# Raw weight tiles into larger free slots, three buffers for q, k and v, loads in written order, ScalarE's decoding in program order

## The chip, the cores and the metric

The kernel runs on one core of a Trainium2 chip. The metric is device time in microseconds (us): the median of three runs, with the lowest and the highest. The profile is of one further execution.

Five engines share the work: TensorE (PE, with its weight loads as PEld), VectorE (DVE), ScalarE (ACT), GpSimd (POOL) and SyncE (SP), which here only issues the DMAs. Each takes its instructions in the order in which the built program has them.

## The reference

Attention over 4 batches of 8 heads, 576 positions of 64 values each. A score is kept where it is within tau = 0.02 of its row's largest; the rest get weight 0. Then two matrix products of a gated layer, one more, and a second layer of two:

```python
scores = scale * np.matmul(q, k.transpose(0, 1, 3, 2))
thresh = np.max(scores, axis=-1, keepdims=True) - tau
scores = np.where(scores >= thresh, scores, -1000000000.0)
scores = scores - np.max(scores, axis=-1, keepdims=True)
attn = np.exp(scores)
attn = attn / (np.sum(attn, axis=-1, keepdims=True) + 1e-09)
x = np.matmul(attn, v)          # then heads side by side: 2304 x 512
...
h = (x @ w1) * (x @ w2) @ w3    # 512 -> 1024, then 1024 x 1024
x = h @ w_out                   # 1024 -> 512
...
h = x @ w_in                    # 512 -> 2048
out = np.maximum(0.01 * h, h) @ w_out2
```

All of it is float32. The weights reach the core as 64-bit integers that hold float64 bits: their size in memory is twice that of float32.

## The kernel before

**Weights.** A weight tile of 128 partitions by 1024 values is loaded in two *halves* of 512 KB (`st`, three buffers) and decoded to float32. ScalarE scales the high words (`t`, L140) and the low words (`st` in place, L141), VectorE shifts `t` left by three bits (L142), GpSimd adds the two (L145, or L148 into `wt`). A weight for a float32r product is then split in two parts: ScalarE rounds (L149) and GpSimd subtracts (L150). `stream` (L108) issues a staging load for each half that has been decoded; it is called for `first` and later for `w2`. The 20 tiles of `first` are four of `wo`, eight of `w3` and eight of `w12`. The 16 of `w2` follow when attention is over.

**Folding.** `fold_weights` (L338) multiplies `w3` and `wo` into `w34` while attention runs: eight blocks of eight products (`ps34`, L346), a block for each tile of `w3`. With `w34` the gated layer needs two products, `psab` (x by `w12`, L367) and `psh` (L386), both float32r with three passes.

**Attention.** A *unit* is a pair of heads of a batch and one of two groups of rows, g = 0 with two steps or g = 1 with three, of which the first has one head's work for both. There are 8 units in a batch, 32 in all, and 80 steps. A unit's q and k lie in `qk`, its v in `vv`, each with two buffers; `load_unit` issues four to six DMAs on SP. `scale_unit` multiplies q on VectorE (L186). A step is `scores` (PE L207 or L211, VectorE's maximum L217, GpSimd's threshold L218, ScalarE's exponential L219), `mask` (VectorE L233), `transposes` (PE L253 to L268, copies by ScalarE and VectorE), and once per unit `weighted` (PE L283) and `normalise` (PE L313, `x` on GpSimd L317).

**Order.** The main loop (L425) walks the steps and puts into each a share of decoding (`halves += 1.7 * weight`, where a step with two heads weighs 2) and of the gated layer (`rate`). The gated layer of a batch's group starts two steps after its last unit. A scheduler then sets the order on each engine from priorities and its own picture of what is ready; the written order counts only where it leaves a tie, for SP's DMAs as well.

**w2.** After attention `stream` decodes the 16 tiles of `w2` into the slots that are free by then; `up` and `down` (L526, L548) run over five chunks of columns, and the rest of the time is theirs.

## Time and profile before

| | |
|---|---|
| median of 3 runs | 1155.42 us (1151.76 to 1160.67) |
| profiled execution | 1158.23 us, span 1156.4 us |
| TensorE busy | 1081.0 us, 93% |
| VectorE, ScalarE, GpSimd busy | 454.6, 474.3, 322.1 us |
| mean granted TensorE clock | 0.980 |
| moved by DMA | 77.61 MB, 223 GB/s in the first fortieth of the span, 46 GB/s in the middle |

The span runs from the first to the last instruction. Busy times of engines overlap; a wait is idle time with the instruction that ended it. A stretch is a window of time from the span's start. The granted clock is a share of TensorE's full speed, 2.4 GHz; a share between 0.5 and 1 means that a part of the stretch ran at the lower level, 1.2 GHz.

### The profile page before, as it was taken

The numbers are of one execution on the slowest core, as the hardware profiler recorded it, in microseconds if no ns is written. First come the engines' busy times: TensorE is split into PE (matmuls) and PEld (weight loads), VectorE is DVE, ScalarE is ACT, GpSimd is POOL, SyncE is SP. The second block draws the span as 40 slices with busy tenths as digits, with TensorE's granted clock in tenths as the row PEclk, the third lists the DMA queues.
The fourth block names the chain that finished last, engine by engine and source line by source line (L and its number), as shares of the span: only waits on it lengthen the run. The fifth ranks groups of instructions, "written<-read, shape, count | busy, mean of one in ns | idle before, by whom it ended". The sixth has DMA issues, their size and how long they took to land.

```text
span 1156.4 us, 16341 instructions
## 1 busy us (share of the span) xinstructions
PE 1081.0 (93%) x6288; PEld 851.8 (74%) x6288; DVE 454.6 (39%) x887; ACT 474.3 (41%) x891; POOL 322.1 (28%) x456
## 2 busy tenths in 40 slices
PE   2799788999999999989999989999999999999998
PEld 1344466778877788877787768987788888888887
DVE  4454555554554554554554554154321121111111
ACT  4545774344343443443443444257632232222232
POOL 3334972122222121221221216388810010000000
PEclk9799799999999999999999998999999999999999
DMA  7544551111211111111121103245320010010000
GB/s 223 163 117 159 170 173 43 46 53 40 67 40 33 54 54 40 53 41 57 41 61 45 40 10 119 70 147 168 111 73 1 1 64 1 1 46 1 1 37 20
DMA packets 37407, 77.61 MB, mean 67 GB/s; under 512 B 4817, under 2 KB 19665, under 8 KB 37329
## 3 DMA queue, kind: packets, MB, share of 16 engines
q1 hardware_dynamic: 37184, 76.56, 21.7%
q8 instruction: 50, 0.82, 0.3%
q14 instruction: 29, 0.23, 0.1%
q10 hardware_dynamic: 144, 0.00, 0.0%
HBM read 67.11 MB, written 9.44 MB: 66 GB/s over the span
## 4 chain that ended last, share of the span: by engine, by line
PE 72%; DMA 9%; DVE 5%; POOL 5%; ACT 4%; issue 3%; SPq 1%; DVEq 0%; ACTq 0%; POOLq 0%
PE po L548 14%; PE ps L526 14%; PE psab L367 13%; PE psh L386 8%; PE av L283 7%; PE sc L211 6%; DMA qk<-in_qkv 4%; DMA st<-in_w 4%; PE tp L263 4%; PE ps L346 2%; POOL wt L148 2%; PE sc L207 1%; DVE nm L217 1%; PE tq L268 1%; DVE t L142 1%
## 5 line engine op out<-in xcount | busy, mean ns | idle before, releaser
L367 PE MATMUL psab<-x,w 128*128 128x256 f32 (+1 forms) x1536 | 233.6, 303 | 4.6 <-DVE xs L314 1.7
L367 PEld LDWEIGHTS psab<-x,w 128*128 128x128 f32 x1536 | 210.0, 190 | 22.4 <-issue 9.9
L526 PE MATMUL ps<-h,w 128*128 128x512 f32 (+1 forms) x960 | 216.0, 370 | 0.4 <-ACT w L149 0.4
L548 PE MATMUL po<-w,gg 128*128 128x512 f32 x864 | 214.1, 392 | 1.9 <-ACT gg L533 1.8
L526 PEld LDWEIGHTS ps<-h,w 128*128 128x128 f32 x960 | 169.5, 188 | 34.9 <-ACT w L149 1.2
L548 PEld LDWEIGHTS po<-w,gg 128*128 128x128 f32 x864 | 159.7, 188 | 38.0 <-ACT gg L533 4.5
L217 DVE TENSOR_REDUCE nm<-sc 128x1 f32<-128x576 f32 x144 | 108.8, 755 | 186.9 <-PE sc L211 144.2
L534 DVE TENSOR_TENSOR gg<-gf,gg 128x512 fp32r<-128x512 f32 (+1 forms) x80 | 60.4, 756 | 268.9 <-ACT gg L533 268.9
L531 ACT ACTIVATE gf<-ps 128x512 f32<-128x512 f32 (+1 forms) x80 | 44.3, 555 | 226.1 <-PE ps L526 226.0
L219 ACT ACTIVATE e<-sc,nm 128x576 f32<-128x576 f32 x144 | 106.9, 742 | 58.8 <-DVE nm L217 56.9
L263 PE MATMUL tp<-ident,e 128*128 128x128 f32 x512 | 80.8, 282 | 43.2 <-DVE e L233 38.8
L233 DVE SCALAR_TENSOR_TENSOR e<-sc,th,e 128x576 f32<-128x576 f32 x144 | 112.4, 812 | 21.0 <-ACT e L219 21.0
L386 PE MATMUL psh<-gt,w 128*128 128x256 f32 (+1 forms) x768 | 112.6, 301 | 1.9 <-ACT xs L286 1.9
L386 PEld LDWEIGHTS psh<-gt,w 128*128 128x128 f32 x768 | 104.0, 190 | 6.7 <-issue 3.5
L263 PEld LDWEIGHTS tp<-ident,e 128*128 128x128 f32 x512 | 61.6, 145 | 55.5 <-issue 33.6
L218 POOL TENSOR_TENSOR th<-cb,nm 128x1 f32<-128x1 f32 x144 | 27.7, 193 | 231.3 <-DVE nm L217 231.3
L211 PE MATMUL sc<-qk 64*128 64x288 f32 x512 | 83.6, 447 | 6.4 <-DVE qk L186 6.0
L142 DVE TENSOR_SCALAR t<-t 128x512 int32<-128x512 int32 x72 | 55.0, 765 | 79.2 <-ACT t L140 69.5
L378 POOL TENSOR_TENSOR gt<-at,gt 128x256 fp32r<-128x256 f32 (+1 forms) x64 | 52.3, 817 | 103.9 <-ACT gt L377 103.8
L283 PE MATMUL av<-HH,vv 128*64 128x256 f32 (+1 forms) x512 | 73.1, 427 | 0.0
L150 POOL TENSOR_TENSOR w<-wt,w 128x512 fp32r<-128x512 f32 x48 | 66.5, 1400 | 20.4 <-ACT w L149 19.8
L503 POOL TENSOR_TENSOR h<-hr,h 128x1024 fp32r<-128x1024 f32 (+1 forms) x10 | 22.3, 2233 | 173.1 <-DVE h L502 173.1
(67 smaller groups left out, 997.7 us busy)
## 6 DMA issues: line engine op xcount, KB each, us to landing
st<-in_w SPq DMA_DIRECT2D x48, 512.0 KB, 4.3
vv<-in_qkv SPq DMA_DIRECT2D x64, 160.0 KB, 2.3
st<-in_w3t SPq DMA_DIRECT2D x16, 512.0 KB, 3.9
qk<-in_qkv SPq DMA_DIRECT2D x32, 208.0 KB, 3.5
qk<-in_qkv SPq DMA_DIRECT2D x32, 144.0 KB, 2.9
out<-os SPq DMA_DIRECT2D x18, 256.0 KB, 2.2
st<-in_wout SPq DMA_DIRECT2D x8, 512.0 KB, 6.4
hr<-h3d SPq DMA_DIRECT2D x8, 512.0 KB, 3.7
```

Source lines behind the costliest of these rows:

```text
L142: nc.vector.tensor_scalar(out=t, in0=t, scalar1=3, scalar2=None, op0=ALU.logical_shift_left)
L150: nc.gpsimd.tensor_tensor(out=dst[:, 1, sl], in0=f(w), in1=f(dst[:, 0, sl]), op=ALU.subtract)
L211: nc.tensor.matmul(sc[:, a, half, :HS], qk[r, o:o + P], qk[r, ks], start=True, stop=True)
L217: nc.vector.tensor_reduce(out=nm, in_=sc[:, a, :, :HS], op=ALU.max, axis=AX.XY, negate=True)
L219: nc.scalar.activation(e[:, a].rearrange("p (a b) -> p a b", a=2), sc[:, a, :, :HS], AF.Exp, bias=nm)
L233: nc.vector.scalar_tensor_tensor(out=ev, in0=sc[:, a, :, :HS], scalar=th, in1=ev, op0=ALU.is_ge, op1=ALU.mult, accum_out=stat[key][:, o:o ...
L263: nc.tensor.transpose(tp[:, kc], e[:, a, kc * P:kc * P + P], ident)
L283: nc.tensor.matmul(av[a * D:a * D + D, :gw], vv[:, a, kc], rhs, start=(i == 0), stop=(i == NK - 1))
L367: nc.tensor.matmul(ps[:, :gw], w12_t[i][:, a, o:o + P], xt[kk][:, c, :gw], start=(m == 0), stop=(m == 11))
L386: nc.tensor.matmul(ps[:, :gw], w34_t[i // 2][:, a, i % 2, o * P:o * P + P], gt[i][:, c, :gw], start=(m == 0), stop=(m == 23))
L526: nc.tensor.matmul(ps[:, :tw], w2_t[j][:, a, kk * P:kk * P + P], h3_t[ci][:, c, kk, :tw], start=(m == 0), stop=(m == 11))
L548: nc.tensor.matmul(po_t[t], gg[:, c, t * P:t * P + P], w2_t[j][:, a, 512:], start=(j == 0 and (a, c) == PASSES[0]), stop=(j == KF2 - 1 and ...
```

## The change

- The halves of `wo`, `w3` and the first four tiles of `w12` are loaded as whole tiles of 1 MB (`raw`) into slots of `wpool` that are free at the time: tag wB for `wo` and `w3`, wA for `w12`. Up to seven halves beyond the decoded ones are asked for. The last four tiles of `w12`, and `w2`, go through `st` as before.
- The low words get a tile of their own (`lw`); `wt` is gone.
- The float32 tiles of `wo` lie in two slots of wA, `w3` has three buffers instead of two, `qk` and `vv` three.
- Up to the gated layer of the first batch's second group, SP's DMAs keep the written order. `load_unit` is called two units ahead.
- The two decoding instructions on ScalarE are held in program order, and the two halves that were decoded ahead of the first scores are not. The pace of decoding is 1.2 instead of 1.7 halves per unit of weight.
- For `w2`, VectorE does the second half's subtraction, and the tiles are assigned to other slots: the fourth lies in a slot of wB instead of a pool that opens later.

```diff
--- before.py
+++ after.py
@@ -105,51 +105,64 @@
         nc.vector.tensor_tensor(out=cb, in0=cb, in1=neg, op=ALU.subtract)
 
 
-    def stream(jobs, pool, depth):
-        ahead = []
-        todo = [(slot, src, c) for slot, src in jobs for c in range(2)]
-        def issue():
-            if todo:
-                slot, src, c = todo.pop(0)
-                st = pool.tile([P, 1024], I32, tag="st", name="st", bufs=depth)
-                nc.sync.dma_start(out=st, in_=src[:, c * 512:c * 512 + 512].bitcast(I32))
-                ahead.append((slot, c, st))
-        for _ in range(depth):
-            issue()
-        return decode(ahead, issue, pool)
-    def decode(ahead, issue, pool):
-        while ahead:
-            slot, c, st = ahead.pop(0)
-            if c == 0:
-                dst = slot()
-            sl = slice(c * 512, c * 512 + 512)
-            words = st.rearrange("p (c two) -> p c two", two=2)
-            low, high = words[:, :, 0], words[:, :, 1]
-            t = pool.tile([P, 512], I32, tag="t", name="t", bufs=2)
-            nc.scalar.activation(f(t), f(high), AF.Prelu, scale=2.0 ** -112, alpha=-2.0 ** 32)
-            nc.scalar.activation(low, low.bitcast(U32), AF.Copy, scale=2.0 ** -29)
-            nc.vector.tensor_scalar(
-                out=t, in0=t, scalar1=3, scalar2=None, op0=ALU.logical_shift_left)
-            if len(dst.shape) == 2:
-                nc.gpsimd.tensor_tensor(out=dst[:, sl].bitcast(I32), in0=t, in1=low, op=ALU.add)
-            else:
-                w = pool.tile([P, 512], I32, tag="wt", name="wt", bufs=2)
-                nc.gpsimd.tensor_tensor(out=w, in0=t, in1=low, op=ALU.add)
-                nc.scalar.copy(dst[:, 0, sl], f(w))
-                nc.gpsimd.tensor_tensor(out=dst[:, 1, sl], in0=f(w), in1=f(dst[:, 0, sl]), op=ALU.subtract)
-            issue()
-            yield
+    def stream(jobs, by_dve):
+        todo = [(job, c) for job in jobs for c in range(2)]
+        loaded = []
+        state = [0, None]
+        def issue(most=2 * len(jobs)):
+            while len(loaded) < min(most, len(todo)):
+                (slot, src, raw), c = todo[len(loaded)]
+                if len(loaded) >= state[0] + (7 if raw in ("wB", "wC") else 3):
+                    return
+                if raw is None:
+                    st = wld.tile([P, 1024], I32, tag="st", name="st", bufs=3)
+                    nc.sync.dma_start(out=st, in_=src[:, c * 512:c * 512 + 512].bitcast(I32))
+                    loaded.append(st)
+                else:
+                    if c == 0:
+                        state[1] = wpool.tile(
+                            [P, 2, 1024], I32, tag="wB" if raw == "wB" else "wA", name="raw")
+                        nc.sync.dma_start(
+                            out=state[1].rearrange("p c w -> p (c w)"), in_=src.bitcast(I32))
+                    loaded.append(state[1][:, c])
+        def decode():
+            for k, ((slot, src, raw), c) in enumerate(todo):
+                if c == 0:
+                    dst = slot()
+                sl = slice(c * 512, c * 512 + 512)
+                words = loaded[k].rearrange("p (w two) -> p w two", two=2)
+                low, high = words[:, :, 0], words[:, :, 1]
+                t = wld.tile([P, 512], I32, tag="t", name="t", bufs=2)
+                lw = wld.tile([P, 512], I32, tag="lw", name="lw", bufs=2)
+                tc.keep_in_program_order(
+                    nc.scalar.activation(f(t), f(high), AF.Prelu, scale=2.0 ** -112, alpha=-2.0 ** 32))
+                tc.keep_in_program_order(
+                    nc.scalar.activation(lw, low.bitcast(U32), AF.Copy, scale=2.0 ** -29))
+                nc.vector.tensor_scalar(
+                    out=t, in0=t, scalar1=3, scalar2=None, op0=ALU.logical_shift_left)
+                if len(dst.shape) == 2:
+                    nc.gpsimd.tensor_tensor(out=dst[:, sl].bitcast(I32), in0=t, in1=lw, op=ALU.add)
+                else:
+                    nc.gpsimd.tensor_tensor(out=lw, in0=t, in1=lw, op=ALU.add)
+                    nc.scalar.copy(dst[:, 0, sl], f(lw))
+                    eng = nc.vector if by_dve and c else nc.gpsimd
+                    eng.tensor_tensor(out=dst[:, 1, sl], in0=f(lw), in1=f(dst[:, 0, sl]), op=ALU.subtract)
+                state[0] = k + 1
+                yield
+                issue()
+        return decode(), issue
 
     units = [(b * 4 + p, g) for b in range(B) for g in range(2) for p in range(4)]
     qk_t, vv_t = {}, {}
@@ -161,8 +174,8 @@
         pair, g = units[u]
         gq, gw, _ = GROUPS[g]
         b, h = pair // 4, 2 * (pair % 4)
-        qk = apool.tile([P, S + 320], F32, tag="qk", name="qk", bufs=2)
-        vv = apool.tile([P, 2, NK, D], F32, tag="vv", name="vv", bufs=2)
+        qk = apool.tile([P, S + 320], F32, tag="qk", name="qk", bufs=3)
+        vv = apool.tile([P, 2, NK, D], F32, tag="vv", name="vv", bufs=3)
         for a in range(2):
             o = a * D
             src = qkv[b, h + a][o:o + D]
@@ -323,17 +336,21 @@
 
     def slot(table, i, tag, name):
         def make():
-            if tag in ("wA", "wB"):
+            if tag == "w3":
+                table[i] = fold.tile([P, 1024], F32, tag=tag, name=name, bufs=3)
+            elif name == "wo":
+                if i % 2 == 0:
+                    table["both"] = wpool.tile([P, 2, 1024], F32, tag=tag, name=name)
+                table[i] = table["both"][:, i % 2]
+            else:
                 table[i] = wpool.tile([P, 2, 1024], F32R, tag=tag, name=name)
-            else:
-                table[i] = fold.tile([P, 1024], F32, tag=tag, name=name, bufs=4 if tag == "wo" else 2)
             return table[i]
         return make
 
-    first = [(slot(wo_t, t, "wo", "wo"), wout[t]) for t in range(4)]
-    first += [(slot(w3_t, i, "w3", "w3"), w3t[i]) for i in range(KF)]
-    first.insert(2, first.pop(4))
-    first += [(slot(w12_t, i, "wB" if i < 4 else "wA", "w12"), w12[i]) for i in range(KF)]
+    first = [(slot(wo_t, t, "wA", "wo"), wout[t], "wB") for t in range(4)]
+    first += [(slot(w3_t, i, "w3", "w3"), w3t[i], "wB") for i in range(KF)]
+    first += [(slot(w12_t, i, "wB" if i < 4 else "wA", "w12"), w12[i],
+               ("wC", "wA", None, None)[i // 2]) for i in range(KF)]
 
     def fold_weights():
 
@@ -363,9 +380,8 @@
                 m = 0
                 for kk in range(KD):
                     for a, c in PASSES:
-                        o = mat * 512 + kk * P
                         nc.tensor.matmul(
-                            ps[:, :gw], w12_t[i][:, a, o:o + P], xt[kk][:, c, :gw],
+                            ps[:, :gw], w12_t[i][:, a, mat * 512 + kk * P:mat * 512 + kk * P + P], xt[kk][:, c, :gw],
                             start=(m == 0), stop=(m == 11))
                         m += 1
                 if mat == 0:
@@ -399,10 +415,15 @@
             yield from gn
 
 
+    in_order = ExitStack()
+    in_order.enter_context(tc.manual_schedule(engines={mybir.EngineType.SP}))
     load_tau()
     load_unit(0)
+    loads, issue = stream(first, False)
+    issue(2)
+    load_unit(1)
+    issue()
     scale_unit(0)
-    loads = stream(first, wld, 3)
     halves_in = [0]
 
     def load_halves(k):
@@ -418,7 +439,6 @@
                 return
 
     folding = fold_weights()
-    load_halves(2)
     scores(0)
     late = {}
     halves = 0.0
@@ -431,7 +451,7 @@
         weight = 1 if c is None else 2
         mask(n)
         if n == 0 or STEPS[n - 1][:2] != (pair, g):
-            load_unit(u + 1)
+            load_unit(u + 2)
         if STEPS[(n + 1) % NS][:2] != (pair, g):
             scale_unit(u + 1)
         if n + 1 < NS:
@@ -452,7 +472,7 @@
         with ahead_of(20):
             for item in late.pop(n, []):
                 item()
-        halves += 1.7 * weight
+        halves += 1.2 * weight
         load_halves(int(halves))
         halves -= int(halves)
         if queue and queue[0][0] == n:
@@ -465,6 +485,10 @@
                 s_ld.close()
                 gpool = s_ffn.enter_context(tc.tile_pool(name="gpool", bufs=8, reuse_waits="tile"))
                 fpool = s_ffn.enter_context(tc.tile_pool(name="fpool", bufs=2, reuse_waits="tile"))
+            if (b, gg) == (0, 1):
+                while halves_in[0] < 40:
+                    load_halves(1)
+                in_order.close()
             filler = gated(b, gg)
             rate, due = (1.22, 1.55)[gg], 0.0
     for n in sorted(late):
@@ -480,14 +504,14 @@
 
     def w2_slot(j):
         def make():
-            if j < 4:
-                w2_t[j] = (p2 if j < 3 else p3).tile([P, 2, 1024], F32R, tag=f"w2_{j}", name="w2", bufs=1)
-            else:
-                w2_t[j] = wpool.tile([P, 2, 1024], F32R, tag=("", "wB", "wA", "w34")[j // 4], name="w2")
+            tag = (f"w2_{j}", "wB", "wA", "w34")[(j + 1) // 4] if j < 15 else "w2_15"
+            pool = wpool if 3 <= j < 15 else (p2 if j < 3 else p3)
+            w2_t[j] = pool.tile([P, 2, 1024], F32R, tag=tag, name="w2", bufs=4 if 3 <= j < 15 else 1)
             return w2_t[j]
         return make
 
-    loads = stream([(w2_slot(j), w2[j]) for j in range(KF2)], wld, 3)
+    loads, issue = stream([(w2_slot(j), w2[j], None) for j in range(KF2)], True)
+    issue()
 
     CH = [(c * 512, 512) for c in range(4)] + [(2048, 256)]
     h3_t = {}
```

**ScalarE, from its first instruction.** `t` and `st` (now `lw`) are decoding, `e` the exponential of a step's head, `HH` and `tl` copies of transposed weights of attention. Before:

```order
L140 ACT_TABLE_LOAD
L140 ACTIVATE t<-st 128x512
L141 ACTIVATE st<-st 128x512
L140 ACTIVATE t<-st 128x512
L141 ACTIVATE st<-st 128x512
L140 ACTIVATE t<-st 128x512
L141 ACTIVATE st<-st 128x512
L219 ACTIVATE e<-sc,nm 128x576 x2
L140 ACTIVATE t<-st 128x512
L141 ACTIVATE st<-st 128x512
```

Now:

```order
L232 ACT_TABLE_LOAD
L232 ACTIVATE e<-sc,nm 128x576 x2
L280 COPY HH<-tp 128x4x128
L282 COPY tl_95<-tq 64x2x128
L149 ACTIVATE t<-raw 128x512
L151 ACTIVATE lw<-raw 128x512
L149 ACTIVATE t<-raw 128x512
L151 ACTIVATE lw<-raw 128x512
L232 ACTIVATE e<-sc,nm 128x576 x2
L280 COPY HH<-tp 128x4x128
```

The first step's exponentials and copies now stand ahead of all decoding; before, six decoding instructions stood ahead of them.

**SP, the loads from the start.** `qk` and `vv` belong to attention; a set of them is a unit's, and units are counted from 0. Before:

```order
L170 DMA qk<-in_qkv 64x832 x2
L175 DMA vv<-in_qkv 128x320 x2
L124 DMA st<-in_wout 128x1024 x3
L170 DMA qk<-in_qkv 64x832 x2
L175 DMA vv<-in_qkv 128x320 x2
L124 DMA st<-in_wout 128x1024
L124 DMA st<-in_w3t 128x1024 x2
L124 DMA st<-in_wout 128x1024 x2
L170 DMA qk<-in_qkv 64x832
L124 DMA st<-in_wout 128x1024
L170 DMA qk<-in_qkv 64x832
L124 DMA st<-in_wout 128x1024
```

Now, from the first weight load to unit 4's:

```order
L135 DMA raw<-in_wout 128x2048
L183 DMA qk<-in_qkv 64x832 x2
L188 DMA vv<-in_qkv 128x320 x2
L135 DMA raw<-in_wout 128x2048 x3
L183 DMA qk<-in_qkv 64x832 x2
L188 DMA vv<-in_qkv 128x320 x2
L135 DMA raw<-in_w3t 128x2048
L183 DMA qk<-in_qkv 64x832 x2
L188 DMA vv<-in_qkv 128x320 x2
L135 DMA raw<-in_w3t 128x2048 x3
L185 DMA qk<-in_qkv 64x576
L186 DMA qk<-in_qkv 64x320
```

A unit's loads were mixed with single halves; now each unit's stand together, behind one to three whole tiles. The next ones follow the same pattern: unit 5 behind two tiles of `w3`, unit 6 behind two of `w3` and one of `w12`, unit 7 behind three of `w12`, unit 8 behind five `st`.

**VectorE, in the second step's place.** `nm` is the maximum of a head's scores, `qk` the scaling of a unit's q. Now:

```order
L230 TENSOR_REDUCE nm<-sc 128x1
L246 SCALAR_TENSOR_TENSOR e,stat<-sc,th,e 128x576 x2
L230 TENSOR_REDUCE nm<-sc 128x1
L278 COPY HH<-tp 128x4x128
L152 TENSOR_SCALAR t<-t 128x512
L199 TENSOR_SCALAR qk<-qk,scl 128x256
L152 TENSOR_SCALAR t<-t 128x512
L230 TENSOR_REDUCE nm<-sc 128x1
L246 SCALAR_TENSOR_TENSOR e,stat<-sc,th,e 128x576 x2
```

The `qk` scaling in these rows is unit 2's and stands ahead of a maximum of the second step. Before, unit 2's stood behind the second step's two masks. From there on each unit's scaling stands, now as before, a few instructions ahead of a maximum or a mask of a unit before it.

**TensorE, at the end of folding.** `ps` are fold blocks, `sc` scores, `psab` the first gated products. Before:

```order
L211 MATMUL sc<-qk 128x288 x4
L254 MATMUL tq<-ident,e 128x128
L263 MATMUL tp<-ident,e 128x128 x4
L253 MATMUL tp<-ident,e 128x128 x4
L283 MATMUL av<-HH,vv 64x256 x8
L268 MATMUL tq<-ident,e 128x128
L263 MATMUL tp<-ident,e 128x128 x4
L211 MATMUL sc<-qk 128x288 x4
L268 MATMUL tq<-ident,e 128x128
L367 MATMUL psab<-x,w_756 128x256 x15
```

Now:

```order
L363 MATMUL ps_859<-wo,w_845 128x512 x8
L276 MATMUL tp<-ident,e 128x128 x4
L224 MATMUL sc<-qk 128x288 x4
L267 MATMUL tq<-ident,e 128x128
L266 MATMUL tp<-ident,e 128x128 x4
L363 MATMUL ps_883<-wo,w_870 128x512 x8
L281 MATMUL tq<-ident,e 128x128
L383 MATMUL psab<-x,w_915 128x256 x2
L224 MATMUL sc<-qk 128x288 x4
L281 MATMUL tq<-ident,e 128x128
L383 MATMUL psab<-x,w_915 128x256 x22
```

Before, the last fold block stands six rows ahead of this piece, with nine score steps ahead of it and two more between it and the first `psab`. Now thirteen score steps stand ahead of the last fold block, and `psab` follows it at once.

## Rows read from the trace of the kernel before

**Rows 1.** The page's first part: busy us, share of span, instructions.

```profile
PE 1081.0 (93%) x6288; PEld 851.8 (74%) x6288; DVE 454.6 (39%) x887; ACT 474.3 (41%) x891; POOL 322.1 (28%) x456
```

**Rows 2.** Busy times by stretch: length; engines' busy us (instructions); clock, DMA share, GB/s.

```profile
0.00:46.00 46.00, 17.04 (x55) 9.08 (x56) 20.50 (x52) 24.37 (x40) 17.90 (x25) 0.81 0.73 213
46.00:114.00 68.00, 66.81 (x258) 32.72 (x256) 31.07 (x63) 31.00 (x55) 24.43 (x33) 1.00 0.44 130
114.00:144.00 30.00, 21.79 (x81) 11.37 (x82) 14.86 (x27) 23.32 (x44) 26.45 (x25) 0.77 0.56 182
144.00:200.00 56.00, 45.81 (x322) 36.11 (x321) 30.79 (x64) 33.56 (x66) 29.01 (x43) 0.97 0.37 112
200.00:680.00 480.00, 464.42 (x3307) 374.27 (x3308) 245.74 (x538) 197.18 (x389) 104.56 (x244) 1.00 0.16 46
...
760.00:840.00 80.00, 77.76 (x328) 60.71 (x327) 37.38 (x38) 52.94 (x94) 70.37 (x50) 1.00 0.47 150
```

**Rows 3.** Busy times of three short stretches, same columns.

```profile
116.00:121.00 5.00, 4.07 (x6) 1.85 (x7) 2.21 (x4) 4.81 (x10) 5.00 (x5) 0.66 0.32 104
130.00:141.00 11.00, 8.57 (x35) 4.83 (x35) 7.37 (x14) 7.47 (x14) 10.82 (x12) 0.53 0.56 173
178.00:182.00 4.00, 3.92 (x16) 3.01 (x17) 2.00 (x6) 1.10 (x3) 1.53 (x5) 0.57 0.03 6
```

**Rows 4.** Timeline, VectorE: start us, us, instruction, [idle before, and what ended it].

```profile
13.58 0.43 DVE L142 TENSOR_SCALAR t<-t 128x512 int32<-128x512 int32 x1 [1.29 <-ACT t L140]
15.05 0.57 DVE L186 TENSOR_SCALAR qk<-qk,scl 128x256 f32<-128x256 f32 x1 [1.04 <-DMA qk<-in_qkv]
...
30.35 0.82 DVE L233 SCALAR_TENSOR_TENSOR e<-sc,th,e 128x576 f32<-128x576 f32 x1 [0.83 <-ACT e L219]
```

**Rows 5.** The view of waits, whole span: total us, times, longest.

```profile
ACT t L140 <- DMA st<-in_wout: 14.6, 6, 6.3
```

**Rows 6.** The chain of waits: start us, us, what it ran through.

```profile
53.91 6.99 DMA qk<-in_qkv
...
65.65 7.11 PE ps L346 x16
...
170.44 1.70 PE psab L367 x12
172.14 0.44 PE tp L263 x4
...
172.68 1.17 PE sc L211 x8
...
184.32 2.30 PE av L283 x16
```

**Rows 7.** Busy times of two stretches of 2 us, columns as before.

```profile
8.00:10.00 2.00, 0.32 (x2) 0.00 (x0) 0.43 (x1) 1.22 (x2) 0.00 (x0) 1.00 1.00 387
...
12.00:14.00 2.00, 0.00 (x0) 0.00 (x0) 0.71 (x2) 1.10 (x2) 1.19 (x2) 1.00 1.08 209
```

**Rows 8.** The page's DMA issues: count, KB each, median us to landing.

```profile
st<-in_w SPq DMA_DIRECT2D x48, 512.0 KB, 4.3
...
qk<-in_qkv SPq DMA_DIRECT2D x32, 208.0 KB, 3.5
```

**Rows 9.** Groups by line, GpSimd, 114 to 200 us: busy, mean ns | idle before.

```profile
L148 POOL TENSOR_TENSOR wt<-t,st 128x512 int32<-128x512 int32 x16 | 21.2, 1329 | 3.1 <-ACT st L141 2.1 <-DVE t L142 0.5 <-ACT gt L377 0.5
L150 POOL TENSOR_TENSOR w<-wt,w 128x512 fp32r<-128x512 f32 x16 | 20.9, 1316 | 3.1 <-ACT w L149 3.1
```

**Rows 10.** Chain of waits at 352 us, and two stretches at such landings.

```profile
352.84 3.54 DMA qk<-in_qkv
...
355.00:358.00 3.00, 1.07 (x10) 0.90 (x10) 2.22 (x6) 1.11 (x2) 0.86 (x2) 1.00 0.10 26
513.00:516.00 3.00, 1.20 (x11) 1.03 (x10) 2.35 (x6) 1.24 (x3) 0.88 (x2) 1.00 0.14 46
```

**Rows 11.** Timeline at 709 us, VectorE.

```profile
709.51 2.68 DVE L142 TENSOR_SCALAR t<-t 128x512 int32<-128x512 int32 x1
```

## What I expect of the change, before it ran

> **What bounds the kernel now.** I read the page's busy times first: TensorE is busy 1081.0 us of a span of 1156.4 [rows 1]. Its work is the same before and after, so all that can be won is its idle time, 75 us, and what it loses at the lower clock level. The second view, busy times by stretch, says where that lies [rows 2]: 46 − 17.04 = 29.0 us idle before 46 us, 1.2 between 46 and 114, 8.2 and 10.2 in the next two stretches, 15.6 in the 480 us of steady state, 2.2 in 760 to 840. In 114 to 144 GpSimd is busy 26.45 of 30 us: there it is the bound, and TensorE waits for it. The clock view adds that TensorE ran mostly at the 1.2 GHz level in three short stretches there (granted 0.66, 0.53, 0.57) after it had stood idle [rows 3]. Half of the low share of its busy time is the loss: 4.07 × (1 − 0.66)/0.5/2 = 1.4, and so 4.0 and 1.7, together 7.1 us.
>
> The timeline and the chain name the waits behind these numbers. At the start unit 1's q (counted from 0) is scaled at 15.05, and the second step's first mask runs at 30.35 [rows 4]; between them ScalarE's exponentials stand behind decodes that wait for staging loads, 14.6 us in six waits for wout alone [rows 5].
>
> The profiled execution took 1158.2 us with 1.8 around its span. That is 2.8 above the median of the three runs, 1155.4. The sum is made against 1158.2.
>
> **Start, 0 to 46 us: −6 us.** ScalarE's order now has two exponentials, two copies, and only then a decode; a decode can no longer hold the first steps. Two loads set what is left. Unit 1's q stands behind 1 MB of weights instead of 1.5; at 387 GB/s, the rate while weights alone move [rows 7], 0.5 MB is 1.4 us, so it lands about 13.6. Its step then needs a reduction, an exponential and a mask: masks at about 16. VectorE next meets the scaling of unit 2's q, placed ahead of the second step's last reduction. That load stands behind everything before it: three sets of q, k at 0.43 MB, two of v at 0.33, 4.2 MB of weights. Weights at 387 GB/s are 10.8 us, the other 1.95 MB at 209 GB/s [rows 7] 9.3; from about 2 us on, it lands near 22. Two reductions, exponential and masks at 0.75 to 0.82 each bring the second step's masks to 25.5, against 30.35 + 1.6 = 32. So 6 us, with 0 (both loads as late as now) and 12 (neither waited for) as ends.
>
> **Folding, 46 us to its end: +4 us.** Weight products cost the same, 7.11 us per block of eight [rows 6], and ScalarE, VectorE and GpSimd had half their time free there [rows 2]. The new cost is SP's order. In the rows of SP, units 4, 5 and 6 each stand directly behind a 1 MB load whose slot comes free only when ScalarE has read an older one. Behind such a DMA wait the q, k and v of that unit and all later weights; VectorE meets the scaling of that q a few instructions later, ahead of reductions that attention needs, and TensorE waits for those. A 1 MB load at 387 GB/s is 2.7 us, and q, k take 3.5 from issue to landing [rows 8]: a bit over 6 us after the decode. VectorE gets there some 3 us after it. So three waits of 3.5, of which a fold block of 7.11 us covers rather more than half: 4 us are left. Ends: 0 (all covered), 12 (none, and longer).
>
> **Decoding w12, 114 to 200 us: −12.5 us.** Today this stretch loses 8.2 + 10.2 idle and 7.1 at the low level, 25.5. The 16 halves cost GpSimd 16 × (1.33 + 1.32) = 42.4 us [rows 9], and its small work in the two stretches is 26.45 + 29.01 − 21.2 − 20.9 = 13.4, 56 in all; at the density of 26.45 in 30 this takes 63 us, before as after. What changes is what TensorE has to do meanwhile. Before, nine score steps stand ahead of the last fold block and two more ahead of the first gated product; after, thirteen, and gated products follow at once. GpSimd starts on w12 while two fold blocks, 14.2 us, still run, so 49 us of its time is exposed. TensorE has 16 gated blocks of 1.70, 27 us, and eight steps of attention: scores 1.17, transposes 0.44 each, 2.30 and its tail for a unit's weighted sums [rows 6], 2.7 to 3.4 a step, 26 in all. 53 against 49: TensorE is the bound by a little, and for the places where it isn't I charge 2 us. Then come units 7, 8 and 9, whose loads stand behind raw w12 or behind staging loads that wait for decodes: three waits of 3.5, here on the binding path, 11 us. So 13 lost instead of 25.5. Ends: 3 lost (waits covered, −22), 30 lost (GpSimd starts late, +5).
>
> **Steady state: −3.7 us.** A load into one of two q buffers goes out when TensorE has let go of it and lands 3.54 us later; the scaling, and behind it the masks, wait. In windows around two such landings TensorE is busy 1.07 and 1.20 of 3 us [rows 10]: 1.9 + 1.8. With a third buffer the load leaves a whole unit earlier, and that covers it. If the cover fails nothing is lost beyond today.
>
> **w2: −1 us.** TensorE idles 2.2 us in 760 to 840, where GpSimd is busy 70.37 of 80 us [rows 2]; the change gives VectorE one of each two subtractions, and loads the fourth w2 tile earlier. A row speaks against a full gain: a shift on VectorE that takes 0.43 us while GpSimd stands idle [rows 4] took 2.68 us while GpSimd subtracted [rows 11]. So the engines do not simply add here; I take 1 us, with +1 and −2.2 as ends. The Trainium skill, in "SBUF — State Buffer", section "Who interferes with whom", says why it should be less: a VectorE instruction with two SBUF inputs and a GpSimd one that reads SBUF hold one shared pair in turn, each for its whole length. By that rule the moved subtractions would still queue with GpSimd's and this term would be 0; the 2.68 us row agrees.
>
> The end of attention stays: the same steps stand there in the same order. Three edits I cost at nothing: the separate low-word tile has the same two adds, wo in one tile of two is the same bytes, and the slower pace of decoding is in the counts above.
>
> The sum: −6 + 4 − 12.5 − 3.7 − 1 = −19.2, so 1139.0 for the profiled execution, and 2.8 less, **1136**, for a median.
>
> **Rivals.**
> - *The waits are covered.* If the fold blocks and GpSimd's backlog hide all the waits for q, 4 + 11 us more are won: 1121. For it speaks that ScalarE and VectorE are under half busy in 46 to 114 [rows 2]; against it, that VectorE takes its instructions strictly in order.
> - *GpSimd binds as before.* w12's third and fourth tiles need slots that wo holds to the last fold block, so its decoding may begin no earlier than today relative to the gated products. Then the third term is 0 and the others give −6.7: 1149. That 26.45 of 30 us are busy speaks for it; that two raw tiles have free slots early speaks against it. That "4 MB ahead" doesn't come about, since most loads wait for a slot in SP's order, ends here too.
> - *SP's head holds attention up.* Units 4 to 9 each have their load behind one that waits for a slot. If none is covered and each costs a whole weight landing, 4.3 us at half the size [rows 8], and 3.5 for q, k, that is 7.8 × 6 = 47 us instead of the 15 charged: 1136 + 32 = 1168, slower than before. It decides from about 5.7 us a unit on, (19.2 + 15)/6. Today's chain has one such wait, 6.99 us at 53.91 [rows 6], and TensorE had fold blocks through it, idle 1.2 us in all of 46 to 114: that speaks against.
>
> **How the numbers follow.** The forecast has 0.58 with a range of its own of 1124 to 1149, covered waits 0.16, GpSimd binding 0.15, SP's head 0.11. The range reaches from 1114, at the sum of all good ends, up to 1158, past the GpSimd case; SP's head and the far ends are left out, about 0.2. The three runs lie within 0.8%, so 1% is about what can be told from no change: under 1143.9 is faster, over 1167 slower. Faster takes 0.52 of the forecast and the covered waits, 0.68; within 1% the rest of the forecast, GpSimd binding and a part of SP's head, 0.22; slower 0.10.
>
> **What would show it.** Right: the second step's masks near 25 us; TensorE over 95% busy between fold start and the first psh; psab starting within a few us of the last fold block; no 3.5 us q landings ahead of the masks after 200 us. Wrong: waits of VectorE's scaling for q, k loads of 5 us and more at units 4 to 9, with TensorE idle in them; a GpSimd under 80% busy while gated products wait for w12; or the first 46 us as idle as before. The forecast falls if these waits add up to more than 34 us.

## The result, and the profile after

The changed kernel took **1167.12 us** (median of 4 runs, 1165.37 to 1170.52) beside 1155.23 us for the kernel before. The ratio is 1.0102, with a 95% interval of 1.0056 to 1.0149: slower by a small amount, where 1136 and faster had been forecast. The profiled execution has a span of 1164.2 us, 7.8 more than before.

First the busy times of the changed kernel by stretch, beside [rows 2]: length; each engine's busy us (instructions); granted clock, DMA share, GB/s.

```profile
0.00:46.00 46.00, 18.41 (x91) 11.34 (x93) 23.70 (x58) 21.14 (x36) 14.20 (x25) 0.84 0.74 243
46.00:114.00 68.00, 60.42 (x235) 29.91 (x236) 30.94 (x61) 26.32 (x47) 19.09 (x32) 0.93 0.35 112
114.00:144.00 30.00, 28.32 (x97) 13.92 (x97) 16.23 (x32) 17.97 (x32) 12.90 (x16) 1.00 0.18 56
144.00:200.00 56.00, 43.43 (x251) 29.89 (x250) 26.28 (x52) 32.12 (x62) 35.07 (x41) 0.88 0.38 126
200.00:230.00 30.00, 21.32 (x121) 14.18 (x120) 13.17 (x25) 14.62 (x28) 14.99 (x19) 0.83 0.32 96
...
760.00:840.00 80.00, 79.94 (x359) 65.33 (x358) 56.02 (x52) 57.51 (x104) 56.34 (x39) 1.00 0.52 170
```

The losses that are new: between 46 and 114 us TensorE is idle 7.6 us instead of 1.2 (from 114 to 144 it is 1.7 instead of 8.2, which makes up for it), and from 144 to 230 it is idle 21.3 us instead of 10.9. GpSimd, which I had as the bound of decoding, is busy 12.90 of 30 us and 35.07 of 56: nobody gives it work.

Why, the instructions of the decode's first ScalarE line show (the view of one line: what ended the idle time of its engine ahead of it: us, times), up to 230 us. Before:

```profile
  DMA st<-in_wout: 14.6, 6
  DMA st<-in_w: 10.5, 6
  DMA st<-in_w3t: 6.2, 4
```

In the changed kernel:

```profile
L149 ACT ACTIVATE t<-raw x32: 647/670/695, 18.8 to 174.6; 128x512 f32<-128x512 f32 x32
its engine sat idle before it (us, times) until:
  POOL wo L155: 0.5, 1
```

Before, ScalarE stood 31 us ahead of decodes, waiting for loads. Now it never waits for one there: the weights have landed. But the decode stands in program order behind each step's exponentials and copies, so it comes when attention has come that far. The last half of w12 is decoded here, on ScalarE's timeline of the changed kernel:

```profile
214.32 0.74 ACT L232 ACTIVATE e<-sc,nm 128x576 f32<-128x576 f32 x1 [1.82 <-DVE nm L230]
...
218.66 0.41 ACT L393 CAST gt<-at 128x256 fp32r<-128x256 f32 x1 [2.04 <-DVE at L391]
218.97 0.66 ACT L149 ACTIVATE t<-st 128x512 f32<-128x512 f32 x1
...
222.12 0.66 ACT L149 ACTIVATE t<-st 128x512 f32<-128x512 f32 x1
```

ScalarE sits idle 1.82 us for a row maximum and 2.04 for a product, and only then come the decodes, at 218.97 and 222.12. Before, the last half was decoded at 156.06:

```profile
156.06 0.66 ACT L140 ACTIVATE t<-st 128x512 f32<-128x512 f32 x1
```

TensorE pays for it, as in these rows of the chain of waits of the changed kernel (start us, us, what):

```profile
219.07 0.58 ACT t L149
219.66 0.50 DVE t L152
220.30 1.27 POOL lw L157
221.59 0.63 ACT w L158
222.26 0.58 PE psab L383
```

Sorted by what ended them, TensorE's own waits between 144 and 230 us say that this is the smaller part (total us, times, longest):

```profile
PE tq L281 <- DVE e L246: 11.1, 4, 3.8
PE psab L383 <- ACT w L158: 5.8, 6, 2.1
```

It stood 5.8 us for weights that ScalarE rounds and 11.1 us for masks of attention. Two of the four waits for masks, at 205.9 and 215.0 us, begin where the gated products at hand have run out and the next one waits for a half that isn't decoded; so late weights take away the work that fills waits for masks. That they explain all 11.1 us is not shown.

For the comparisons below I count one number per stretch, an estimate from the rows: TensorE's idle time plus its busy time × (1 − granted clock), the rule that the prediction used for the low level. For the kernel before, the rows of the wider stretches are:

```profile
46.00:144.00 98.00, 88.60 (x339) 44.09 (x338) 45.94 (x90) 54.32 (x98) 50.89 (x57) 0.93 0.47 146
144.00:230.00 86.00, 75.06 (x541) 59.03 (x540) 46.27 (x98) 44.77 (x87) 33.88 (x56) 0.98 0.29 88
230.00:680.00 450.00, 435.17 (x3090) 351.36 (x3089) 230.26 (x504) 185.97 (x368) 99.69 (x231) 1.00 0.16 46
```

So 144 to 230 cost (86 − 75.06) + 75.06 × 0.02 = 12.4 us before. The same for all profiled executions that matter, in us lost:

| kernel | 0-46 | 46-144 | 144-230 | 230-680 | 680-840 | last w12 half decoded at |
|---|---|---|---|---|---|---|
| before | 32.2 | 15.6 | 12.4 | 14.8 | 10.0 | 156.1 |
| changed | 30.5 | 13.7 | 30.3 | 11.6 | 9.2 | 222.1 |
| changed, SyncE free | 27.6 | 9.3 | 31.0 | 13.2 | 8.1 | 219.4 |
| changed, ScalarE free | 25.0 | 13.8 | 18.4 | 16.9 | 13.2 | 182.8 |
| the same, w2's decode kept | 27.1 | 15.6 | 17.4 | 16.1 | 8.1 | 185.4 |
| that and SyncE free | 25.2 | 10.2 | 7.6 | 22.8 | 3.0 | 146.3 |
| that and scaling placed early | 25.6 | 9.6 | 3.2 | 19.4 | 0.7 | 145.6 |
| before, decode kept | 23.9 | 15.7 | 27.3 | 14.6 | 12.4 | 182.0 |

The clock is given to two digits, so a figure of the longest stretch is good to about 2 us, and the sums agree with the spans to about 5. The whole loss of the change, 18 us, lies in one stretch, 144 to 230 us; the other stretches won 8 us back. (Where the expectations give 153.8 and 181 us for the last half of w12, these are the half before it.)

### The profile page after: what moved, and what is told of

Same layout as the page of the kernel before. It is cut to its first block, busy times and chain, and to the rows that moved or that the text cites. A ratio compares the mean times of both kernels' runs of the same rounds, so it can differ in the third digit from the quotient of the medians.

```text
span 1164.2 us, 16221 instructions
## 1 busy us (share of the span) xinstructions
PE 1084.4 (93%) x6288; PEld 855.5 (73%) x6288; DVE 475.1 (41%) x903; ACT 470.2 (40%) x891; POOL 299.5 (26%) x440
## 4 chain that ended last, share of the span: by engine, by line
PE 76%; DMA 7%; DVE 6%; ACT 5%; POOL 2%; issue 2%; SPq 1%; DVEq 0%; ACTq 0%; POOLq 0%
PE po L572 16%; PE ps L550 16%; PE psab L383 13%; PE psh L402 8%; PE av L296 7%; DMA qk<-in_qkv 6%; PE sc L224 5%; PE tp L276 4%; PE ps L363 3%; DVE nm L230 2%; ACT e L232 2%; PE sc L220 1%; DVE e L246 1%; PE tq L281 1%; ACT t L149 1%
## 5 line engine op out<-in xcount | busy, mean ns | idle before, releaser
L383 PE MATMUL psab<-x,w 128*128 128x256 f32 (+1 forms) x1536 | 238.4, 304 | 9.3 <-ACT w L158 5.8
L558 DVE TENSOR_TENSOR gg<-gf,gg 128x512 fp32r<-128x512 f32 (+1 forms) x80 | 64.2, 804 | 254.7 <-ACT gg L557 254.7
L157 POOL TENSOR_TENSOR lw<-t,lw 128x512 int32<-128x512 int32 x48 | 67.2, 1410 | 15.6 <-ACT lw L151 7.9
L363 PE MATMUL ps<-wo,w 128*128 128x512 f32 x128 | 60.8, 622 | 8.9 <-POOL w L155 8.8
```

The lines of the kernel that those rows point to most:

```text
L157: nc.gpsimd.tensor_tensor(out=lw, in0=t, in1=lw, op=ALU.add)
L363: nc.tensor.matmul(ps, w3_t[i][:, j * P:j * P + P], wo_t[j // 2][:, (j % 2) * 512:(j % 2) * 512 + 512], start=(j == 0), stop=(j == KF - 1))
L383: nc.tensor.matmul(ps[:, :gw], w12_t[i][:, a, mat * 512 + kk * P:mat * 512 + kk * P + P], xt[kk][:, c, :gw], start=(m == 0), stop=(m == 11))
```

## The experiments

Two theories were on record. **A**: SyncE's written order holds attention up, since q, k, v stand behind loads that wait for slots. **B**: ScalarE's program order delivers the weights late, whoever loads them. A third, **C**, on the third buffer, came with the second batch. Each batch shared its runs of the kernel before (medians 1156.6, 1157.56 and 1155.19), so ratios are compared, not times.

### SyncE's order taken back

```diff
-    in_order.enter_context(tc.manual_schedule(engines={mybir.EngineType.SP}))
-                in_order.close()
```

> The changed kernel with SyncE's loads no longer in written order; the scheduler sorts them as before the change. Theory A (the q, k and v of units 2 to 9 stand in SyncE's queue behind weight or v loads that wait for a slot, and TensorE waits with them): VectorE's waits for q at units 4 to 9, 21 us together in the changed kernel (4.69, 1.22, 8.10, 1.79, 1.66, 2.54, and 3.33 at unit 10), fall under 10, and the time to 1145 to 1156. Theory B (decoding, kept behind attention on ScalarE and paced at 1.2 halves, delivers the weights late, whoever loads them): the waits for decoded halves stay and the time is 1162 to 1170.

1166.03 us, ratio 1.0076 (1.0047 to 1.0106): not told apart from the changed kernel's 1.0102. VectorE's waits for q at units 4 to 10 fell from 23.3 us to 13.3, not under the 10 that was expected, yet 144 to 230 lost 31.0 us, no less than the changed kernel's 30.3, and w12's last half was decoded at 219.4. Its rows there:

```profile
144.00:230.00 86.00, 63.99 (x378) 45.27 (x378) 38.82 (x78) 46.08 (x89) 47.86 (x56) 0.86 0.25 79
```

Theory A, as the cause by itself, falls; theory B's figure holds.

### ScalarE's order taken back

```diff
-                tc.keep_in_program_order(
-                    nc.scalar.activation(f(t), f(high), AF.Prelu, ...))
+                nc.scalar.activation(f(t), f(high), AF.Prelu, ...)
...
-                tc.keep_in_program_order(
-                    nc.scalar.activation(lw, low.bitcast(U32), AF.Copy, scale=2.0 ** -29))
+                nc.scalar.activation(lw, low.bitcast(U32), AF.Copy, scale=2.0 ** -29)
```

> The changed kernel with the decode's two ScalarE instructions placed by the scheduler again, not in program order; SyncE stays in written order. Theory A: the blocked loads stay, 1162 to 1172; if decodes move ahead of exponentials and wait there for loads, up to 1180. Theory B: fold blocks and gated products get their halves earlier, TensorE's idle time between 46 and 230 us falls from 29 to under 18 us, 1148 to 1157.

1161.18 us, 1.0026 (1.0000 to 1.0053), below the changed kernel's interval. 144 to 230 lost 18.4 us instead of 30.3; TensorE's idle time between 46 and 230 fell from 30.5 us to 21.0, not under the 18 that was expected. The median missed theory B's 1148 to 1157, and two stretches show where: 680 to 840 lost 13.2 instead of 9.2 (w2's decodes now stand among the copies of the last gated products; the run with w2's decode kept tests this), and 144 to 230 was still 6 us worse than before.

### q, k and v through ScalarE's queue

```diff
+        eng = nc.sync if u < 2 else nc.scalar
...
-                nc.sync.dma_start(out=qk[o:o + D, :S + gw], in_=src[:, :S + gw])
+                eng.dma_start(out=qk[o:o + D, :S + gw], in_=src[:, :S + gw])
...
         nc.scalar.copy(xs[:, :gw], av[:, :gw])
         xs_t[pair, g] = xs
+        load_v(units.index((pair, g)) + 3, nc.scalar)
```

> The changed kernel with q, k and v from unit 2 on issued by ScalarE's queue (v directly behind the copy that frees its slot); SyncE keeps the weights alone, in the same written order. Theory A: no q waits behind a weight load and no weight load behind v; VectorE's waits for q at units 4 to 9 under 8 us in all, TensorE's idle time between 46 and 230 us from 29 to under 18, 1146 to 1156. Theory B: weights are decoded at the same places as now, so 1162 to 1170. Against both: the 0.5 us per issue on ScalarE, some six per unit, could cost up to 3 us per unit while ScalarE paces the decode.

1171.09 us, 1.0116 (1.0076 to 1.0156). Inconclusive about A: the loads left SyncE's queue, but stood in ScalarE's, where each again came when attention had come that far. VectorE's waits for q stayed at 31.1 us in all (40.1 in the changed kernel), and ScalarE, which issued loads first, ran its first exponential at 12.9 us instead of 9.1.

### The pace back at 1.7

```diff
-        halves += 1.2 * weight
+        halves += 1.7 * weight
```

> The changed kernel with the pace of decoding back at 1.7 halves per step half instead of 1.2; all else as changed. Theory A: the loads wait in SyncE's queue for the same slots, a little earlier, 1160 to 1170. Theory B: the last fold block stands fewer score steps back, w12 is decoded sooner, 1147 to 1157.

1163.11 us, 1.0048 (1.0020 to 1.0075). The time lies in the range that theory A gave and not in B's, but its interval overlaps with the changed kernel's, so it does not decide. The trace leans to B: w12's last half came at 196.4 instead of 222.1, and 144 to 230 lost 18.6.

### w2's decode alone kept in order

```diff
+        keep = tc.keep_in_program_order if by_dve else (lambda x: x)
...
-                tc.keep_in_program_order(
+                keep(
```

> The changed kernel with the decode's ScalarE instructions free for the scheduler while wo, w3 and w12 are decoded, and in program order for w2 alone; SyncE in written order. Theory B (decoding kept behind attention starves folding and the gated products): as the run with all decodes free between 46 and 230 us, and as the changed kernel from 680 us on, where that run lost 4 us; 1150 to 1158. Theory A (SyncE's order decides): 1160 to 1168.

1152.23 us, 0.9940 (0.9916 to 0.9965): faster than before, as B had it, and 0.0162 below the changed kernel. 680 to 840 lost 8.1 us, so keeping the order pays for w2 and harms wo, w3 and w12. Now ScalarE waits for loads again:

```profile
its engine sat idle before it (us, times) until:
  DMA raw<-in_w3t: 20.4, 6
  DMA raw<-in_wout: 8.5, 2
...
```

And SyncE's own waits between 40 and 130 us say why the raw tiles are late (columns: total us, times, longest):

```profile
SPq L189 <- PE tq L282: 28.9, 1, 28.9
SPq L189 <- PE bc L327: 22.5, 1, 22.5
SPq L189 <- PE av L297: 20.1, 1, 20.1
```

L189 loads v. Its slot comes free only when a unit's weighted sums are through, and the next raw tiles stand behind it. So SyncE's written order does block, but in this run through v holding up the weights, 71.5 us in three waits, and not mainly through the weights holding up q, as theory A and my third rival had it.

### That, and SyncE's order taken back

The diffs of the first and the last run above, together.

> The run before this one with SyncE's written order taken back too. If SyncE's order is a second limit behind ScalarE's (in the run with free decodes the decodes came in bursts: 26.8 to 42.0, 51.3 to 69.2, 107.5 to 126.0, 138.0 to 156.7 us, where raw tiles were late), then w12's last half is decoded before 165 us instead of 181, and the time is 4 to 10 us lower than that of the run before: 1143 to 1152. If SyncE's order costs nothing by itself, both take the same time within 2 us.

1138.33 us, 0.9817 (0.9780 to 0.9854), better than expected. Taking SyncE's order back is worth 0.0123 of the time here, 14 us, where it was worth 0.0026, within the intervals, while ScalarE's order stood: the two limits lie one behind the other. On SyncE's timeline the last two raw tiles of w3 leave at 49.17 us:

```profile
49.17 0.81 SPq L136 DMA_DIRECT2D raw<-in_w3t  x2
```

In the run before they left at 88.04. The stretch now reads

```profile
144.00:230.00 86.00, 80.03 (x582) 63.74 (x579) 45.67 (x96) 39.26 (x77) 26.57 (x48) 0.98 0.21 65
```

### The scaling of q in program order

```diff
-        nc.vector.tensor_scalar(out=q, in0=q, scalar1=scl, ...)
+        tc.keep_in_program_order(
+            nc.vector.tensor_scalar(out=q, in0=q, scalar1=scl, ...))
```

> The run before this one with VectorE's scaling of q in program order. Theory C (the third q buffer sends the load a unit earlier, but the scheduler moves the scaling up with it, so VectorE still stands at its landing): with the scaling kept where it is written, one unit later, no wait for q over 0.5 us is left after 230 us, and the stretch from 230 to 680 us loses 4 to 8 us less; 3 to 8 us less than the run before. If the landings were never what attention waited for, no difference within 2 us.

1151.41 us, 0.9937 (0.9915 to 0.9960): 13 us slower than the run before, where 3 to 8 faster were expected. Half of theory C held: VectorE waits for q once, at unit 0, against 12 times (14.5 us) in the run before.

```profile
DVE qk L201 <- DMA qk<-in_qkv: 1.4, 1, 1.4
```

The other half did not: 230 to 680 lost 34.0 us instead of 22.8. VectorE's timeline shows what came in the landing's place:

```profile
315.08 0.82 DVE L248 SCALAR_TENSOR_TENSOR e<-sc,th,e 128x576 f32<-128x576 f32 x1 [0.88 <-ACT e L234]
...
316.57 0.39 DVE L201 TENSOR_SCALAR qk<-qk,scl 128x320 f32<-128x320 f32 x1
```

and TensorE's, in the same place:

```profile
316.06 0.63 PE L278 MATMUL tp<-ident,e 128*128 128x128 f32 x4 [3.24 <-DVE e L248]
...
317.85 1.14 PE L222 MATMUL sc<-qk,qz 128*128 128x288 f32 x4
```

The loads of this unit's q and k had left by 267.8, and such loads took at most 3.5 us to land there; but the scaling is written behind two masks, at 316.57. So the scores of the next unit, at 317.85, could not fill the 3.24 us in which TensorE waited for those masks.

### The kernel before, with the decode kept in order

```diff
-            nc.scalar.activation(f(t), f(high), AF.Prelu, ...)
-            nc.scalar.activation(low, low.bitcast(U32), AF.Copy, scale=2.0 ** -29)
+            tc.keep_in_program_order(
+                nc.scalar.activation(f(t), f(high), AF.Prelu, ...))
+            tc.keep_in_program_order(
+                nc.scalar.activation(low, low.bitcast(U32), AF.Copy, scale=2.0 ** -29))
```

> The kernel before with one part of the change alone: the decode's two ScalarE instructions in program order. Theory B: decodes come later, w12's last half after 180 us instead of 153.8, 1162 to 1176. Theory A, and any theory by which buffers or SyncE's order made the loss: SyncE is still free here, no change, 1152 to 1160.

1169.16 us, 1.0092 (1.0056 to 1.0127): this one part, alone, makes a slowdown as large as the whole change's. The loss lies in the same stretch, 27.3 us instead of 12.4:

```profile
144.00:230.00 86.00, 68.29 (x447) 54.67 (x448) 45.17 (x85) 47.20 (x91) 47.10 (x62) 0.86 0.35 111
```

But the way there isn't late weights alone. The last half of w12 is decoded at 182.0, as in the run with ScalarE free (182.8), which lost only 18.4 us. TensorE never waits for a weight in this stretch here; its long waits are for masks:

```profile
PE tp L265 <- DVE e L235: 13.0, 3, 5.0
```

Before, waits for that came to 5.1 us in two. The chain into the longest of them, which ends at 148.34, runs through ScalarE's decodes, ahead of the exponential that attention needs:

```profile
145.34 0.54 ACT t L141
145.89 0.56 ACT st L143
146.45 0.25 ACT at L375
146.70 0.65 ACT e L221
```

So the order costs in both directions: decodes wait for attention's steps, and attention's steps wait for decodes. How the loss divides between the two was not measured.

### The scaling in order, but a unit's length earlier

```diff
             load_unit(u + 2)
-        if STEPS[(n + 1) % NS][:2] != (pair, g):
             scale_unit(u + 1)
```

> As the run with the scaling in program order (w2's decode alone kept, SyncE free), but the scaling of unit u+1 written at unit u's first step instead of its last. Theory C (there the third buffer hid every landing, and what TensorE lost instead, 61.8 us between 230 and 680 against 51.7, was four gaps of 3.2 us and smaller ones where scores waited for a scaling that stood behind masks): with the scaling a unit's length ahead of its scores both waits are gone, and that stretch loses under 46 us; 1128 to 1136 against 1138 for the scheduler's place. If those gaps had another cause they stay: 1145 to 1153.

**1125.66 us, 0.9744 (0.9720 to 0.9767)**: the best version. The wait for q is gone as in the run with the late scaling, and of the run's four gaps of 3.2 us in steady state three are 1.2 now (the fourth, near 665 us, is 3.5). Its row for 144 to 230, and below it 230 to 680:

```profile
144.00:230.00 86.00, 84.52 (x616) 67.41 (x612) 45.18 (x98) 40.50 (x81) 26.14 (x49) 0.98 0.22 67
230.00:680.00 450.00, 434.93 (x3096) 351.24 (x3095) 229.35 (x500) 186.69 (x369) 101.19 (x232) 0.99 0.15 44
```

The expectation counted that second stretch in another way, with 61.8 us lost for 2975 of TensorE's instructions in one run and 51.7 for 3054 in the other; scaled by these, 3096 instructions make about 46, an estimate, at the edge of what was expected. In the table's count it is 19.4 against 22.8 with the scheduler's place, a gain of 3.4, and 4.4 more lie in 144 to 230. Whether this version needs the third buffer was not tried.

### Pace, w2's subtractions and buffers, from the better version

All three start from the version of 1138 us: the pace back at 1.7; `eng = nc.gpsimd` for all of w2's subtractions; two buffers for q, k and v with

```diff
-            load_unit(u + 2)
+            if u:
+                load_unit(u + 1)
```

> As the best run so far (w2's decode alone kept, SyncE free, 1138) with the pace back at 1.7. Theory B says that the pace matters where the decode is kept in the written order, since there it sets the place: with the order free the time moves by less than 4 us, 1134 to 1142. If the pace had a share of its own, its sign in the changed kernel (4 us faster at 1.7) should return: 1131 to 1135.

1140.70 us, 0.9873 (0.9859 to 0.9888): a little slower than 0.9817, just clear of its interval. So the pace of 1.2 costs no time once the order is free.

> As the best run so far, with all of w2's subtractions on GpSimd as before the change. If VectorE's share made the gain after 680 us, GpSimd paces w2 again, TensorE idles by 2 to 6 us there: 1140 to 1144. If the gain came from w2's slots and loads, no change: 1136 to 1140.

1140.95 us, 0.9872 (0.9843 to 0.9902). The time leans to 6 us for VectorE's share, but the intervals overlap; the trace gives 158.55 − 156.42 = 2.1 us of TensorE's time in 680 to 840, with GpSimd busy 110.34 instead of 92.29, and names a wait of that size which the version of 1138 us doesn't have:

```profile
PE ps L549 <- POOL w L161: 2.1, 6, 0.5
```

> As the best run so far, with two buffers for q, k and v, loaded one unit ahead. Theory C: as the scheduler places the scaling, the third buffer hides no landing in steady state, so only the decoding stretch can lose: 1137 to 1146. If the third buffer carried the gain, 1150 to 1158.

1133.80 us, 0.9816 (0.9801 to 0.9830): the same as with three. As the scheduler places the scaling, the third buffer is worth nothing.

## Why the prediction was wrong, point by point

**Start, −6 forecast, −1.7 measured.** The mechanism held to half a microsecond. The second step's masks, forecast near 25.5, in the changed kernel's VectorE timeline:

```profile
25.08 0.82 DVE L246 SCALAR_TENSOR_TENSOR e<-sc,th,e 128x576 f32<-128x576 f32 x1 [0.88 <-ACT e L232]
```

But TensorE had little to do with the time won: its first fold block starts at 49.5 us instead of 41.0. The pace of 1.2 puts it there. With ScalarE's order free the block's ten halves are added up by 30.8 us, and it starts at 49.1 all the same; with the pace of 1.7 as well (the run of 1140.70 us) it starts at 30.6. The prediction took the pace for costless.

**Folding and w12, +4 and −12.5 forecast, +16.0 measured** (13.7 + 30.3 against 15.6 + 12.4). This is the step that failed: "GpSimd starts on w12 while two fold blocks, 14.2 us, still run", and then "53 against 49", a race of TensorE against GpSimd. ScalarE was not in that sum. In the changed kernel GpSimd's first addition for w12 is this one:

```profile
140.83 1.26 POOL L157 TENSOR_TENSOR lw<-t,lw 128x512 int32<-128x512 int32 x1
```

The last fold block ends at 145.0, so 4 us of it still run and not 14.2; and the sixteen halves then last until 227.3 on GpSimd, 86 us for the 63 forecast, and it is busy in only 52.5 of them. I had read ScalarE's new order in the first 46 us, for what it takes off attention, and not in the next 180, for what it does to the decode. The rows were there: ScalarE's 31 us of waiting ahead of decodes [rows 5, and the rows above] meant that decodes ran ahead of attention as soon as data came; in program order each runs at attention's pace. GpSimd as the bound of the stretch was misread already in the kernel before: of its chain of waits between 112 and 146 us, 51% is the landing of staging loads for w12, and GpSimd's own work about a sixth. GpSimd 58% busy between 144 and 230 (35.07 + 14.99 of 86 us), while gated products wait, is the sign that the prediction itself named as the one against it.

**The rival that matched, for the wrong reason.** "SP's head holds attention up" gave 1168 and the measured time is 1167: the right number by luck. Without that order the time stays at 1.0076. Its waits are real, 23.3 us on VectorE, but lay beside the wait for decodes; only with ScalarE free does the same order cost 14 us. The other rival that named decoding, "GpSimd binds as before", had the right place and the wrong engine.

**Steady state, −3.7 forecast, −3.2 measured, not by that mechanism.** The waits that the third buffer was to hide are still there between 230 and 680 us (total us, times, longest), in the kernel before and in the changed one:

```profile
DVE qk L186 <- DMA qk<-in_qkv: 9.4, 11, 1.4
DVE qk L199 <- DMA qk<-in_qkv: 11.8, 8, 3.3
```

The load leaves a unit earlier, and the scheduler moves the scaling up with it: unit 12 is scaled at 264.0 us for scores at 304.4, before at 273.8 for 294.1. VectorE stands at the landing as it did. That the run with two buffers takes the same time agrees with it. What the 3.2 us come from was not settled, and they are little above the 2 us that the count of this stretch can tell; the runs with free decodes and the same three buffers lost 16 to 17 us there.

**w2, −1 forecast, −0.8 measured for 680 to 840.** In 760 to 840 TensorE's idle time went from 2.2 us to 0.06, the whole of the good end, and VectorE's share is worth 2.1 us by the run without it. The subtraction on VectorE ran 1.29 us in the mean while GpSimd's ran 1.32, in the version of 1138 us:

```profile
L161 POOL TENSOR_TENSOR w<-lw,w 128x512 fp32r<-128x512 f32 x16 | 21.1, 1317 | 11.1 <-ACT w L159 11.1
L161 DVE TENSOR_TENSOR w<-lw,w 128x512 fp32r<-128x512 f32 x16 | 20.6, 1286 | 8.1 <-ACT w L159 6.6
```

GpSimd then waited 11.1 us for ScalarE ahead of its own: it was no longer the bound. The prediction's reading of the Trainium skill's "Who interferes with whom" in "SBUF — State Buffer" would have made this term 0; the measured 2.1 us decides against that reading. Its mechanism is not refuted, since VectorE's subtraction took 0.68 us at its shortest and 1.56 in the median, in the changed kernel.

**Sum.** Without ScalarE's program order for the first weights and SyncE's written order, the same change lost 10.2 + 7.6 us between 46 and 230 instead of 15.6 + 12.4, −10.2 where −8.5 was forecast. So these two terms were nearly right in their sum for a kernel that lacks two parts of the change, though not each by itself (−5.4 and −4.8). That this kernel took 1138, close to the 1136 forecast, is luck all the same: its steady state lost 8.0 us more than before where 3.7 less were forecast, and 680 to 840 lost 7.0 less where 1 was. (The good ends of the prediction add up to about 1115 and not to 1114; nothing hangs on it.)

## What to carry to other kernels

When an instruction is pinned in program order on a shared engine, ask both ways: what it delays or no longer delays, and what now delays it; the second price falls on whoever waits for its output, here some 100 us after the place where the first was won. A limit that is lifted in front of a second one may gain nothing until the second is lifted too (0.0026 alone, 0.0123 together here), so test such pairs together before calling either harmless. An extra buffer bought nothing here while its consumer moved up with the load; so look where the scheduler puts the consumer, and if you hold it back, not so far that the work it feeds can no longer fill a gap.

## What was not expected of the hardware

A subtraction of two SBUF operands on VectorE, 128x512, took 0.68 us at its shortest and 1.56 us in the median of the 16 in the changed kernel, most of them beside GpSimd's work on SBUF; the shift on one operand took 0.41 us at its shortest and up to 2.61. Sharing such work between the two engines still took 2.1 us of waiting off TensorE for 16 subtractions moved, though the total times don't tell the two runs apart.
